# Opening and closing of the convolution backward: a table loaded in two pieces, k^T chunks summed in another order, and a norm correction that lags two tiles

## The chip, the cores and the metric

The kernel runs on one core of a Trainium2 chip. The metric is the device time of one execution in microseconds. All engines of the core are used: TensorE (PE), VectorE (DVE), ScalarE (ACT), GpSimd (POOL) and SyncE (SP). SP only issues transfers here; ACT and POOL issue some beside their own work.

## The reference, cut to what matters

The program is the forward pass and all gradients of four blocks in a row: a long convolution block, an MLP block, and both once more with the same weights. S = 2048 tokens, D = 512 channels, F = 1376 hidden channels, bfloat16.

```python
def _A_ref(q, k, v, shift_k, ssm_k, ssm_D):          # the convolution block
    k_shift = sum over t of 4: k shifted by (3 - t) tokens * shift_k[:, 3 - t]
    kv = k_shift * v
    y = causal convolution of kv with ssm_k along S (by FFT) + kv * ssm_D
    return q * y

def _B_ref(x, w1, b1, w2, b2):                       # the MLP block
    return gelu(x @ w1 + b1) @ w2 + b2

x = x + _A_ref(_layernorm(x), ...)
x = x + _B_ref(_layernorm(x), ...)
x = x + _A_ref(_layernorm(x), ...)
x = x + _B_ref(_layernorm(x), ...)
return x and its gradients for q, k, v, shift_k, ssm_k, ssm_D, w1, b1, w2, b2
```

(The two functions are given in words where the code is long.) What matters below: the gradient of `shift_k` is, for every channel and each of the four shifts, a sum over all tokens of the gradient of `k_shift` times a shifted `k`. The backward of a layernorm subtracts from the gradient of each token two multiples of simple sums over its 512 channels.

## The kernel before, in words

The program has four stages. The forward convolution fills 0 to about 210 us, the forward MLP runs to about 470 us, the backward of the MLP and the norms to about 640 us, and the last 300 us hold the backward of the convolution together with the weight gradients of the MLP.

**The MLP backward** (`phase_mlp`, `b_bwd`, `a_bwd`) works on four slices of 512 tokens, called lanes. Each lane is a Python generator, and `interleave` takes the lane with the least clock next; in this stage a scheduler then orders the instructions of each engine. Lane 3 is the last, and its layer 1 comes last of its layers of that kind. At the end of `b_bwd` four tiles of 128 tokens go through this: eleven matmuls into `gn_ps` (L1133); DVE takes the dot product of `gn_ps` with the normed input `n`, row by row (L1142, output `bb_junk`, sum in `cols`); POOL writes a diagonal matrix `bb_diag` from it (L1145); PE adds that diagonal times `n` to `gn_ps` (L1137), which is the norm correction; DVE then scales and adds (L1138, output `g_sl`). The correction of tile t - 1 is written behind the matmuls of tile t. `a_bwd` then forms `ab_u` and `ab_p` (L1173, L1167, L1171), POOL makes two columns `ab_ab` (L1177 to L1180), ACT applies them to `nb_sl` (L1182), and DVE adds (L1184), and adds into `gy_bf` (L1186, L1188), from which the convolution's backward starts.

**The convolution backward** (`conv_backward`) is written in a fixed order on PE and DVE (`Ordered` keeps the program's order there). It begins with a forward transform of `gy_bf`: DVE folds it (`Fold`; tiles `fold_s`, `fold_t`, `fold_d`), and PE multiplies by a table `tabFb` of 128 partitions x 2 x 2 x 2048, 2 MB in all, which is loaded from `tabF_d` by one transfer on ACT's queue (L729). The columns of the table are cut into five groups (`GROUPS`, of 2, 2, 4, 4, 4 blocks of 128 columns), and `fwd_group` does one group: matmuls into `sp_ps`, evicted by ACT to `GY` (L314). Then come the products with the stored spectra (`Hb`, `KVb`), inverse transforms (`iv_ps`), and for each of four token blocks the gradients of `k_shift` and `v`: `ksb_b`, `Wb`. PE turns them (`gt_ps`, `gr_ps`), and ACT writes `gksT` (L799) and `gr`, a view of `gy_bf` (L796). PE then forms the gradient of k (`gk_ps`), and DVE forms that of `shift_k`: for each of four channel chunks `cc`, and each shift j and half, one `scalar_tensor_tensor` multiplies `gksT` or `gr` by a chunk of k^T and sums along the row. These are 32 instructions, whose product goes to a spare part of `gy_bf` (so the profile calls them `gy_bf<-gksT,kTc` and `gy_bf<-gy_bf,kTc`). The k^T chunks come from `kT_d` on POOL's queue (L810, 544 KB each): chunks 0 and 1 into the buffers that `vb` used (tag `Sg`), chunk 2 into a spare part of `gy_bf`, chunk 3 into a tile of its own. Last comes the gradient of `ssm_k` (`gh_ps`, `Wh`, `ibh`, `gh`).

**The weight gradients** (`weight_grads`) fill the gaps: `conv_backward` yields an amount of room, and the fill generator is stepped until the room is used. A unit of it is sixteen matmuls `dw_ps` on one 128-channel chunk `dw_tm`. In the first half of the units `dw_tm` is loaded through a transposing DMA on SP's queue (L1231 and L55); in the second half PE turns a loaded `dw_fm` (`dw_tp`), ACT evicts it to `dw_tm` (L1246), and DVE sums the rows of `dw_fm` (`b1a`), after which the buffer of `dw_fm` is free. `dw_fm` and `dw_tm` rotate through seven buffers, and up to five units are fetched ahead. Every instruction that goes through `Ordered` has line 55 in the profile; tiles tell them apart.

Of the kernel before, what the change touches and what calls it, by code (L numbers as in the profile page):

```python
# [13 lines left out]
BF16 = mybir.dt.bfloat16  # L14
F32 = mybir.dt.float32
I32 = mybir.dt.int32
P = 128
# [221 lines left out]
def tok_io(nc, sb, ap2d, flipped, i, store=False, eng=None):  # L239
    eng = eng or nc.sync  # L240
    lo = ap2d[i * 512:i * 512 + 256, :].rearrange("(t p) d -> p t d", p=P)
    hi = flipped[i].rearrange("(t p) d -> p t d", p=P)
    for s, d in ((sb[:, 0:2, :], lo), (sb[:, 2:4, :], hi)):
        last = eng.dma_start(out=d, in_=s) if store else eng.dma_start(out=s, in_=d)
    return last
# [43 lines left out]
        return dict(er=T[:, 0], oi=T[:, 1], nei=T[:, 2], orr=T[:, 3])  # L289


def fwd_group(nc, psum, tab, st, g, out, extra=None, m0=0, m1=None):
    k1, base, n = GROUPS[g]
    for mt in range(m0, n if m1 is None else m1):
        cols = slice((base + mt) * P, (base + mt + 1) * P)
        ps = psum.tile([P, 2, 512], F32, name="sp_ps", tag="sp", bufs=2)
        R, Z = [], []
        for qt in range(2):
            C, S = tab[:, 0, qt, cols], tab[:, 1, qt, cols]
            q = slice(qt * 512, (qt + 1) * 512)  # L300
            if k1 in (0, 4):
                R.append((C, st["e"][:, q]))
                Z.append((S, st["o"][:, q]))
            else:
                R += [(C, st["er"][:, q]), (S, st["oi"][:, q])]
                Z += [(C, st["nei"][:, q]), (S, st["orr"][:, q])]
        if extra is not None:
            er, ez = extra(g, mt, st)
            R += er
            Z += ez  # L310
        for b, lst in ((0, R), (1, Z)):
            for i, (a, r) in enumerate(lst):
                nc.tensor.matmul(ps[:, b, :], lhsT=a, rhs=r, start=(i == 0), stop=(i == len(lst) - 1))
        nc.scalar.activation(out=out[:, :, mt - m0, :], in_=ps, func=ACT.Identity)  # L314
# [393 lines left out]
def conv_backward(ctx, nc, tc, dims, consts, dram, res, aps):  # L708
# [16 lines left out]

    H, KV = load_spec("Hb", dram.Hspec, 0), load_spec("KVb", dram.KVspec, 0)
    with tc.tile_pool(name="cb_tabF", bufs=1, side="right", reuse_waits="tile") as tp:
        tabF = tp.tile([P, 2, 2, 2048], BF16, name="tabFb")
        nc.scalar.dma_start(out=tabF, in_=dram.tabF)  # L729
        fg = Fold(nc, tp, None, None, False, res.gy_bf[:, :, :].rearrange("p (i e h) d -> p e i (h d)", i=4, e=2))  # L730
        yield 14.0
        for g, (k1, base, n) in enumerate(GROUPS):
            fwd_group(nc, psum, tabF, fg.streams(k1), g, GY[g])
    tmp = res.gy_bf[:, :, :].rearrange("p (x a b) d -> p x a b d", x=4, a=2)

    with tc.tile_pool(name="cb_w", bufs=1, side="right", reuse_waits="tile") as wp:
# [26 lines left out]
        with tc.tile_pool(name="cb_io", bufs=1, side="right", reuse_waits="tile") as io:  # L763
# [2 lines left out]
            kc3 = io.tile([P, 4 * 544], BF16, name="kTc3")  # L766
            wdiag = io.tile([P, ND, 4, P], BF16, name="wdiag_b")
            dma(out=wdiag, in_=dram.wdiag)
            ksbs = [io.tile([P, 4, D], BF16, name="ksb_b", tag="ksb", bufs=4) for i in range(4)]
            vbs = []  # L770
            for i in range(4):
# [2 lines left out]
                vbs.append(v2[:, i % 2])  # L774
                dma(out=ksbs[i], in_=dram.ks[:, 4 * i:4 * i + 4, :])
                tok_io(nc, vbs[i], v_ap, dram.vB, i, eng=nc.gpsimd)
            tf = res.gy_bf[:, :, :].rearrange("p t d -> p (t d)")
            gr = tf[:, 0:4096].rearrange("p (c i q) -> p c i q", c=ND, i=4)
            nc.vector.memset(gT[:, :, S:S + 16], 0.0)
            for i in range(4):  # L780
                vb, ksb = vbs[i], ksbs[i]
                for h in range(4):
                    gkv = W[h % 2][:, h // 2, 4 + i, :]
                    tt(out=ksb[:, h, :], in0=gkv, in1=ksb[:, h, :], op=ALU.mult)
                    tt(out=gkv, in0=gkv, in1=vb[:, h, :], op=ALU.mult)
                    ps = psum.tile([P, 2, 512], F32, name="gt_ps", tag="sp", bufs=2)
                    for cc in range(ND):
                        cs = slice(cc * P, (cc + 1) * P)
                        nc.tensor.matmul(ps[:, 0, cs], lhsT=gkv[:, cs], rhs=consts.ident if h < 2 else consts.anti,
                                         start=True, stop=True)  # L790
                    if h >= 2:
                        pr = psum.tile([P, 2, 512], F32, name="gr_ps", tag="sp", bufs=2)
                        for cc in range(ND):
                            cs = slice(cc * P, (cc + 1) * P)
                            nc.tensor.matmul(pr[:, 0, cs], lhsT=gkv[:, cs], rhs=consts.ident, start=True, stop=True)
                        nc.scalar.activation(out=gr[:, :, i, P * (h - 2):P * (h - 1)],  # L796
                                             in_=pr[:, 0, :].rearrange("p (c t) -> p c t", c=ND), func=ACT.Identity)
                    t0 = 512 * i + (P * h if h < 2 else 512 - P * (h - 1))
                    nc.scalar.activation(out=gT[:, :, t0:t0 + P],  # L799
                                         in_=ps[:, 0, :].rearrange("p (c t) -> p c t", c=ND), func=ACT.Identity)  # L800
                yield 3.0
                last = tok_io(nc, ksb, out3, dram.o3B, i, store=True, eng=nc.gpsimd)
                if i % 2:
                    with tc.issue_after(last.ins):
                        unflip_rows(nc, aps[f"out_{i // 2}"].flatten_outer_dims(), (dram.o0B, dram.o1B)[i // 2],
                                    eng=nc.gpsimd)
            kcs = [gyp.tile([P, 4096], BF16, name="kTc", tag="Sg", bufs=2)[:, 0:4 * 544] for cc in range(2)]
            kcs += [tf[:, 4096:4096 + 2176], kc3]
            for cc in range(ND):
                dma(out=kcs[cc], in_=dram.kT[:, cc, :, :].rearrange("p i w -> p (i w)"))  # L810
            unflip_rows(nc, out3, dram.o3B, eng=nc.gpsimd)
            for t in range(NT):
                ps = psum.tile([P, 2, 512], F32, name="gk_ps", tag="sp", bufs=2)
# [7 lines left out]
                if t % 4 == 3:  # L821
                    dma(out=out2[(t - 3) * P:(t + 1) * P, :].rearrange("(t p) d -> p t d", p=P), in_=go)
            junk = tf[:, 6272:6272 + 1024].rearrange("p (i q) -> p i q", i=4)
            for cc in range(ND):
                kc = kcs[cc].rearrange("p (i w) -> p i w", i=4)
                for j in range(4):
                    for half in range(2):
                        if half == 0:
                            g_, k_ = gT[:, cc, 0:S].rearrange("p (i q) -> p i q", i=4)[:, :, 0:256], 16 - j
                        else:  # L830
                            g_ = gr[:, cc]
                            k_ = 272 + j
                        nc.vector.scalar_tensor_tensor(out=junk, in0=g_, scalar=1.0, in1=kc[:, :, k_:k_ + 256],
                                                       op0=ALU.mult, op1=ALU.mult, accum_out=gwo[:, half, cc, j:j + 1])
                    yield 2.2
# [61 lines left out]
TS = 4  # L897
# [206 lines left out]
def b_bwd(nc, m, g, l, s, ret, rows, load=None):  # L1104
# [20 lines left out]
        yield 1.0 * k  # L1125
    go = m.gxpool.tile([P, TS, D], BF16, name="g_sl", tag=f"x{s}", bufs=1)
    cols = m.small.tile([P, 2, TS], F32, name="bb_cols", tag="bb_cols", bufs=4)
    pss = {}
    for t in range(TS + 1):
        if t < TS:  # L1130
            ps = pss[t] = m.psum.tile([P, D], F32, name="gn_ps", tag="oo", bufs=4)
            for c in range(NFC):
                nc.tensor.matmul(ps, lhsT=gz[:, c, t * P:(t + 1) * P], rhs=w.w1T[:, c, :], start=(c == 0),  # L1133
                                 stop=(c == NFC - 1))
        if t > 0:
            u, ps = t - 1, pss.pop(t - 1)
            nc.tensor.matmul(ps, lhsT=dg, rhs=n[:, u, :], start=False, stop=True, skip_group_check=True)  # L1137
            nc.vector.scalar_tensor_tensor(out=go[:, u, :], in0=ps, scalar=m.rstd[l][:, s * TS + u:s * TS + u + 1],  # L1138
                                           in1=g[:, u, :], op0=ALU.mult, op1=ALU.add, accum_out=cols[:, 1, u:u + 1])
        if t < TS:  # L1140
            junk = m.small.tile([P, D], BF16, name="bb_junk", tag="bb_junk", bufs=2)
            nc.vector.scalar_tensor_tensor(out=junk, in0=pss[t], scalar=1.0, in1=n[:, t, :], op0=ALU.mult,  # L1142
                                           op1=ALU.mult, accum_out=cols[:, 0, t:t + 1])
            dg = m.small.tile([P, P], BF16, name="bb_diag", tag="bb_diag", bufs=4)
            nc.gpsimd.tensor_scalar(out=dg, in0=m.ident, scalar1=cols[:, 0, t:t + 1], scalar2=-1.0 / D,  # L1145
                                    op0=ALU.mult, op1=ALU.mult)
        if t == 1:
            n2 = m.spool.tile([P, TS, D], BF16, name="nb_sl", tag="n", bufs=m.n_bufs)
            nc.sync.dma_start(out=n2, in_=tok(m.n_d[l - 1], s))
        yield 2.5 if t < TS else 0.2  # L1150
# [304 lines left out]
```

## Time and profile before

| what | value |
|---|---|
| median of 5 runs | 943.59 us (941.13 to 946.16) |
| the profiled execution | 943.52 us, with a span of 941.7 us |
| instructions | 12144 |
| PE, DVE, ACT, POOL busy | 780.1, 733.7, 568.0, 153.8 us |
| mean granted clock of PE | 0.937 |
| 2 MB table, from issue to landing | 11.05 us |

The profile is of one execution. The span runs from the first to the last instruction, and the rest of the execution's time lies around it. In the rows quoted below the first two numbers are the start and the duration in microseconds; in brackets stands how long the engine had been idle before, and what ended that. Matmuls overlap, so the row of a group of them ends a little after the start of the next.

### The profile page before, as it was taken

What the parts mean: (1) busy time and instruction counts of PE and PEld (TensorE: products, weight loads), DVE (VectorE), ACT (ScalarE), POOL (GpSimd) and SP (SyncE); (2) the same over time, 40 slices, a digit from 0 to 9 for tenths busy, and PEclk for the clock granted to TensorE, in tenths of its full rate; (3) what the DMA queues carried; (4) which work ended last, traced back from release to release, by engine and by line L of the source; (5) the groups of instructions that cost most, each with busy time, mean ns of one, the idle gap of its engine ahead of it and who ended that gap; (6) DMA issues with size and microseconds to landing.
All of it is one profiled execution on the core that took longest, in us unless ns stands there. A gap on an engine that the chain in (4) does not pass through costs nothing.

```text
span 941.7 us, 12144 instructions
## 1 busy us (share of the span) xinstructions
PE 780.1 (83%) x4402; PEld 386.0 (41%) x4402; DVE 733.7 (78%) x1203; ACT 568.0 (60%) x742; POOL 153.8 (16%) x274
## 2 busy tenths in 40 slices
PE   3698878964787759639999999977999998987997
PEld 2463323421333324214444444422444445844664
DVE  7748488896898989766647778896389998499974
ACT  5867644637998879579954545622623238634664
POOL 6632210022002010200001122221011304300000
PEclk9999989977989879879999999977999999999999
DMA  6568786213435453575797986688799897862221
GB/s 218 178 251 319 278 281 233 90 46 89 145 121 160 133 159 125 173 195 158 227 303 230 232 233 188 196 189 191 178 262 243 245 383 256 282 202 79 86 83 39
DMA packets 199668, 180.82 MB, mean 192 GB/s; under 512 B 95733, under 2 KB 182456, under 8 KB 199096
## 3 DMA queue, kind: packets, MB, share of 16 engines
q1 hardware_dynamic: 185320, 133.60, 49.6%
q0 software_dynamic: 11968, 40.15, 12.1%
q10 hardware_dynamic: 2320, 6.29, 1.7%
q8 instruction: 34, 0.56, 0.3%
q14 instruction: 26, 0.21, 0.1%
HBM read 84.22 MB, written 82.13 MB: 177 GB/s over the span
## 4 chain that ended last, share of the span: by engine, by line
PE 44%; DVE 24%; ACT 17%; DMA 6%; issue 5%; POOL 3%; SPq 1%; ACTq 0%; DVEq 0%; POOLq 0%
PE dw_ps L55 10%; PE sp_ps L55 7%; PE gn_ps L1133 7%; PE gh_ps L1115 7%; PE iv_ps L55 4%; DVE gy_bf L55 4%; ACT g_z L1089 3%; DVE b1a L55 3%; ACT g_q L1062 2%; ACT g_s L1065 2%; PE gh_ps L55 2%; ACT g_o L1066 2%; DMA kTc<-kT_d 2%; PE z_ps L1087 2%; ACT n_sl L1009 2%
## 5 line engine op out<-in xcount | busy, mean ns | idle before, releaser
L55 PE MATMUL dw_ps<-G,dw_tm 128*128 128x512 bf16 x704 | 168.1, 387 | 8.9 <-ACT dw_tm L1246 8.9
L1087 PE MATMUL z_ps<-nT_sl,w_sb 128*128 128x512 bf16 x352 | 94.4, 428 | 45.3 <-DMA nT_sl<-n_sl 32.3
L1098 PE MATMUL o_ps<-w_sb,h_sl 128*128 128x512 bf16 x352 | 90.4, 397 | 30.0 <-DVE h_sl L1069 27.4
L55 PEld LDWEIGHTS <-dw_tm 128*128 128x128 bf16 x704 | 67.2, 99 | 82.6 <-ACT dw_tm L1246 11.9
L1117 ACT ACTIVATE gz_sl<-gh_ps 128x512 bf16<-128x512 f32 x88 | 50.3, 594 | 57.3 <-PE gh_ps L1115 54.2
L1133 PE MATMUL gn_ps<-w1T_sb,gz_sl 128*128 128x512 bf16 x352 | 81.2, 379 | 1.2 <-DVE gz_sl L1118 1.2
L1115 PE MATMUL gh_ps<-gT_sl,w2T_sb 128*128 128x512 bf16 x352 | 79.1, 379 | 0.0
L1087 PEld LDWEIGHTS <-w_sb 128*128 128x128 bf16 x352 | 37.4, 108 | 100.1 <-issue 53.9
L1089 ACT ACTIVATE g_z<-z_ps,b1col 128x512 bf16<-128x512 f32 x88 | 55.2, 710 | 27.4 <-PE z_ps L1087 27.4
L1098 PEld LDWEIGHTS <-h_sl 128*128 128x128 bf16 x352 | 34.7, 101 | 78.5 <-DVE h_sl L1069 35.5
L1246 ACT ACTIVATE dw_tm<-dw_tp 128x1024 bf16<-128x1024 bf16 x44 | 44.3, 1023 | 36.0 <-PE dw_tp L55 17.9
L1133 PEld LDWEIGHTS <-gz_sl 128*128 128x128 bf16 x352 | 34.4, 98 | 42.8 <-DVE gz_sl L1118 1.7
L1115 PEld LDWEIGHTS <-w2T_sb 128*128 128x128 bf16 x352 | 34.4, 98 | 41.1
L55 DVE TENSOR_REDUCE b1a<-dw_fm 128x1 f32<-128x2048 bf16 x22 | 49.6, 2278 | 0.0
L989 POOL TENSOR_SCALAR rstd<-ln_mv 128x4 f32<-128x4 f32 x16 | 7.6, 474 | 250.2 <-DVE ln_mv L987 161.7
L1145 POOL TENSOR_SCALAR bb_diag<-ident,bb_cols 128x128 bf16<-128x128 bf16 x32 | 22.0, 686 | 158.6 <-DVE bb_junk L1142 149.4
L1118 DVE TENSOR_TENSOR gz_sl<-gz_sl,gpb 128x2048 bf16<-128x2048 bf16 (+1 forms) x24 | 27.3, 1139 | 23.8 <-DMA gpb<-gp_d 12.3
L1065 ACT ACTIVATE g_s<-g_t 128x2048 bf16<-128x2048 bf16 (+1 forms) x24 | 42.8, 1784 | 2.5 <-DVE g_t L1064 2.4
L1062 ACT ACTIVATE g_q<-g_z 128x2048 bf16<-128x2048 bf16 (+1 forms) x24 | 43.2, 1799 | 0.1
L1069 DVE TENSOR_TENSOR h_sl<-g_s,g_z 128x2048 bf16<-128x2048 bf16 (+1 forms) x24 | 27.2, 1132 | 20.1 <-ACT g_s L1065 20.1
L1066 ACT ACTIVATE g_o<-g_t 128x2048 bf16<-128x2048 bf16 (+1 forms) x24 | 42.7, 1779 | 0.0
L1305 ACT ACTIVATE dw_o<-dw_ps 128x512 bf16<-128x512 f32 x22 | 13.1, 596 | 48.3 <-PE dw_ps L55 28.4
(297 smaller groups left out, 1639.5 us busy)
## 6 DMA issues: line engine op xcount, KB each, us to landing
dw_fm<-gz_d SPq DMA_DIRECT2D x22, 512.0 KB, 7.8
h_d<-h_sl SPq DMA_DIRECT2D x16, 512.0 KB, 2.9
gp_d<-g_p SPq DMA_DIRECT2D x16, 512.0 KB, 3.2
nb_sl<-n_d SPq DMA_DIRECT2D x16, 512.0 KB, 4.6
gpb<-gp_d SPq DMA_DIRECT2D x16, 512.0 KB, 4.3
gz_d<-gz_sl SPq DMA_DIRECT2D x16, 512.0 KB, 5.1
n_d<-n_sl SPq DMA_DIRECT2D x12, 512.0 KB, 3.3
Hspec_d<-Hg ACTq DMA_DIRECT2D x8, 512.0 KB, 5.3
```

The lines of the kernel that those rows point to most:

```text
L55: return self.tc.keep_in_program_order(f(*args, **kwargs))
L1062: nc.scalar.activation(out=q, in_=zb, func=ACT.Square)
L1065: nc.scalar.activation(out=sg, in_=t, func=ACT.Sigmoid)
L1066: nc.scalar.activation(out=o, in_=t, func=ACT.Sigmoid, scale=-1.0)
L1087: nc.tensor.matmul(ps, lhsT=w.w1[:, dc, c * P:(c + 1) * P], rhs=nT[:, dc, :], start=(dc == 0), stop=(dc == ND - 1))
L1089: nc.scalar.activation(out=zb[:, c - c0, :], in_=ps, func=ACT.Identity, bias=w.b1col[:, c:c + 1])
L1098: nc.tensor.matmul(ps, lhsT=h[:, c, t * P:(t + 1) * P], rhs=w.w2[:, c, :], start=(c == 0), stop=False)
L1115: nc.tensor.matmul(ps, lhsT=w.w2T[:, dc, c * P:(c + 1) * P], rhs=gT[:, dc, :], start=(dc == 0), stop=(dc == ND - 1))
L1117: nc.scalar.activation(out=gz[:, c, :], in_=ps, func=ACT.Identity)
L1118: nc.vector.tensor_tensor(out=gz[:, c0:c0 + k, :], in0=gz[:, c0:c0 + k, :], in1=gp[:, 0:k, :], op=ALU.mult)
L1133: nc.tensor.matmul(ps, lhsT=gz[:, c, t * P:(t + 1) * P], rhs=w.w1T[:, c, :], start=(c == 0), stop=(c == NFC - 1))
L1246: nc.scalar.activation(out=dst, in_=ps, func=ACT.Identity)
```

## The change

The change has three parts.

1. The table `tabFb` becomes two tiles: its first 512 columns, which are groups 0 and 1, and the other 1536. Each is loaded by a transfer of its own on ACT's queue. `fwd_group` gets an offset for the columns.
2. The loads of k^T chunks 3 and 2 are written earlier in the program (chunk 3 behind the loads of `vb`, chunk 2 behind the first token block), and the sums run over the chunks in the order 3, 2, 0, 1 in place of 0, 1, 2, 3.
3. In layer 1 of lane 3 the norm correction is written two tiles behind the matmuls in place of one. All other lanes keep one.

```diff
-def fwd_group(nc, psum, tab, st, g, out, extra=None, m0=0, m1=None):
+def fwd_group(nc, psum, tab, st, g, out, extra=None, m0=0, m1=None, c0=0):
...
-        cols = slice((base + mt) * P, (base + mt + 1) * P)
+        cols = slice((base + mt) * P - c0, (base + mt + 1) * P - c0)
...
-        tabF = tp.tile([P, 2, 2, 2048], BF16, name="tabFb")
-        nc.scalar.dma_start(out=tabF, in_=dram.tabF)
+        tabF = []
+        for x, w in ((0, 512), (512, 1536)):
+            tabF.append(tp.tile([P, 2, 2, w], BF16, name=f"tabFb{x}"))
+            nc.scalar.dma_start(out=tabF[-1], in_=dram.tabF[:, :, :, x:x + w])
...
-            fwd_group(nc, psum, tabF, fg.streams(k1), g, GY[g])
+            fwd_group(nc, psum, tabF[g > 1], fg.streams(k1), g, GY[g], c0=0 if g < 2 else 512)
...
+            tf = res.gy_bf[:, :, :].rearrange("p t d -> p (t d)")
+            kcs = [None, None, tf[:, 4096:4096 + 2176], kc3]
+
+            def load_kc(cc):
+                dma(out=kcs[cc], in_=dram.kT[:, cc, :, :].rearrange("p i w -> p (i w)"))
...
-            tf = res.gy_bf[:, :, :].rearrange("p t d -> p (t d)")
+            load_kc(3)
...
                 last = tok_io(nc, ksb, out3, dram.o3B, i, store=True, eng=nc.gpsimd)
+                if i == 0:
+                    load_kc(2)
...
-            kcs = [gyp.tile([P, 4096], BF16, name="kTc", tag="Sg", bufs=2)[:, 0:4 * 544] for cc in range(2)]
-            kcs += [tf[:, 4096:4096 + 2176], kc3]
-            for cc in range(ND):
-                dma(out=kcs[cc], in_=dram.kT[:, cc, :, :].rearrange("p i w -> p (i w)"))
+            for cc in range(2):
+                kcs[cc] = gyp.tile([P, 4096], BF16, name="kTc", tag="Sg", bufs=2)[:, 0:4 * 544]
+                load_kc(cc)
...
-            for cc in range(ND):
+            for cc in (3, 2, 0, 1):
...
-    pss = {}
-    for t in range(TS + 1):
+    pss, dgs = {}, {}
+    lag = 2 if l == 1 and s == 3 else 1
+    for t in range(TS + lag):
...
-        if t > 0:
-            u, ps = t - 1, pss.pop(t - 1)
-            nc.tensor.matmul(ps, lhsT=dg, rhs=n[:, u, :], start=False, stop=True, skip_group_check=True)
+        if t >= lag:
+            u, ps = t - lag, pss.pop(t - lag)
+            nc.tensor.matmul(ps, lhsT=dgs[u], rhs=n[:, u, :], start=False, stop=True, skip_group_check=True)
...
-            dg = m.small.tile([P, P], BF16, name="bb_diag", tag="bb_diag", bufs=4)
+            dg = dgs[t] = m.small.tile([P, P], BF16, name="bb_diag", tag="bb_diag", bufs=4)
```

In the built program POOL issues its transfers in the same order as before, PE changes only in the place of one correction, and on SP's queue the two stores of lane 2's gradient move ahead of one transposing load of `dw_tm`. On DVE the order changes in lane 3's tiles and in the 32 sums.

## The prediction

> **What bounds the kernel now.** The profiled execution took 943.5 us: a span of 941.7 us and 1.8 us around it. It stands at the median of the runs shown (943.59), so the sum is made against it directly. First the page: its busy times and its forty slices of 23.5 us.
>
> ```profile
> span 941.7 us, 12144 instructions
> PE 780.1 (83%) x4402; PEld 386.0 (41%) x4402; DVE 733.7 (78%) x1203; ACT 568.0 (60%) x742; POOL 153.8 (16%) x274
> PE   3698878964787759639999999977999998987997
> PEclk9999989977989879879999999977999999999999
> ```
>
> TensorE and VectorE are close, so neither total decides. The three edits lie in slices 26 to 36 (612 to 870 us). There the busy times by stretch, in the order span, PE, PEld, DVE, ACT, POOL, clock, DMA share, GB/s:
>
> ```profile
> 654.00:690.00 36.00, 35.91 (x153) 15.65 (x154) 16.13 (x33) 17.45 (x18) 2.01 (x3) 0.92 0.83 185
> 690.00:770.00 80.00, 80.00 (x390) 37.04 (x389) 75.29 (x100) 23.44 (x33) 13.77 (x21) 1.00 0.98 282
> 800.00:815.00 15.00, 14.70 (x230) 13.18 (x228) 0.79 (x1) 10.02 (x18) 3.22 (x3) 1.00 0.89 283
> 815.00:840.00 25.00, 22.74 (x206) 14.05 (x204) 24.52 (x34) 12.68 (x17) 4.14 (x5) 1.00 0.86 277
> 840.00:870.00 30.00, 21.86 (x143) 12.39 (x141) 29.55 (x40) 10.83 (x15) 0.18 (x1) 0.89 0.25 72
> ```
>
> From 654 to 770 PE is never idle: what PE starts earlier there ends earlier. At 800 to 815 DVE does nothing; at 815 to 870 DVE is full, and PE is idle for 10.4 us with its clock down. The chain of waits names a transfer at both places:
>
> ```profile
> 642.94 11.05 DMA tabFb<-tabF_d
> 654.04 5.31 PE sp_ps L55 x12
> 660.45 20.88 PE sp_ps L55 x96
> 797.78 16.34 DMA kTc<-kT_d
> ```
>
> Last the timeline (start, us, engine, what, and in brackets the idle time before it and who ended it):
>
> ```profile
> 631.39 0.61 PE L1137 MATMUL gn_ps<-nb_sl,bb_diag 128*128 128x512 bf16 x1 [4.02 <-POOL bb_diag L1145]
> 649.04 2.36 DVE L55 TENSOR_TENSOR fold_t<-fold_s 128x2048 bf16<-128x2048 bf16 x2
> 654.04 6.36 PE L55 MATMUL sp_ps<-fold_t,tabFb 128*128 128x512 bf16 x16 [6.89 <-DMA tabFb<-tabF_d]
> 801.21 0.59 ACT L796 ACTIVATE gy_bf<-gr_ps 128x512 bf16<-128x512 f32 x1
> 814.21 1.23 DVE L55 SCALAR_TENSOR_TENSOR gy_bf<-gksT,kTc 128x1024 bf16<-128x1024 bf16 x1 [17.38 <-DMA kTc<-kT_d]
> 838.37 1.94 ACT L1246 ACTIVATE dw_tm<-dw_tp 128x1024 bf16<-128x1024 bf16 x2 [3.32 <-DVE b1a L55]
> 839.45 0.60 PE L55 MATMUL dw_ps<-G,dw_tm 128*128 128x512 bf16 x2 [2.23 <-ACT dw_tm L1246]
> 868.51 5.50 PE L55 MATMUL gh_ps<-tabG,GY 128*128 128x257 bf16 x48 [2.19 <-ACT Wh L871]
> ```
>
> PE waits for the table although its other operand (the first of the two fold_t) is there at about 650.2. DVE waits for a k^T chunk although gksT and gr are there at 801.8; its row sums (b1a) then come late, these free the buffers for ACT's dw_tm, and PE waits for those.
>
> **The change, part by part.**
>
> *K^T order.* Nothing is added; 32 products with 1.22 us each and the row sums between them keep their count, and the order of issues on POOL's queue comes out the same: chunk 3 was already issued at 749.15 (landing 15.5 us later) and chunk 2 at 767.63 (7.0 us later), both in hand by 775. So the "moved" loads are free, and the whole effect is DVE's order 3, 2, 0, 1. The first product now needs gksT, last written by ACT at 800.71 + 0.60 = 801.3. DVE starts at 801.4 in place of 814.2: 12.8 us. Chunks 0 and 1, landing at 814.1, are needed after sixteen products (16 x 1.26 us) and three row sums (3 x 2.2 us), at 828: hidden, with 14 us to spare. What can PE take of it? It is in the gk_ps block until 818.3 in any case. From there to 868.5 it waited 2.23, 1.66, 1.65 and 2.63 us for dw_tm and 2.19 us for Wh, 10.4 in all, and it lost about 4.5 us to half rate after these waits (seven dw_ps at 840.34 took until 843.15 in place of 841.85, and the like up to 865). So PE could win up to 14.9. DVE's row sums come 12.8 earlier, each then before PE's unpaced need of it, except the last, due about a microsecond late: Wh stands behind it on ACT. I take 12.0 us. From 870 to 936 PE is busy for 64.5 of 66 us on work in a fixed order, so the gain reaches the end.
>
> *Table in two pieces.* Removed: one transfer of 2 MB, 11.05 us. Added: 0.5 MB in runs of 1 KB, and 1.5 MB in runs of 3 KB, each with its issue on ACT's queue (0.35 us; ACT's next work waits 9.94 us for sp_ps anyway, so 0.35 costs nothing; uncovered it would cost just that). New waits: piece one waits, as the whole did, for the sixth dw_tm transpose; piece two also for the DMA of the fourth unit's dw_tm, which PE took at 644.16. Behind this wait on ACT stand only the GY evictions, which wait for PE. The size of the pieces is not in the trace. By the table's own rate piece one is 2.8 us; the nearest rows of 512 KB took 4.6 (nb_sl), 7.0 (wdiag_b) and 13.2 (Hb, the same moment but a queue on POOL). I take 5 us, and keep 2.8 to 13. Issued at 642.9, it lands by 648, ahead of fold_t at 650.2. Piece two at 0.75 x 11.05 = 8.3 us, issued some 0.4 us after its dw_tm has landed, is there at about 653; PE needs it after 6.41 us of the first two groups (654.04 to 660.45), at 656.6. So PE starts at 650.2: 3.8 us.
>
> A rule speaks against this part. The Trainium skill (DMA: Bandwidth & Descriptors, Queues, rings and completion order) says that each DMA engine alternates between queues packet by packet. From 615 to 660 us the trace has 144 packets for 2.10 MB on ACT's queue, about 15 KB a turn, against some 320 B on SP's with the transposes (17808 packets, 5.73 MB); with 1 and 3 KB a turn the table loses share. By the trace's busy shares a transpose packet takes 28 ns (68.4% of 45 us x 16 engines / 17808) and one of the table 0.57 us (11.4% likewise), so 1 KB against one such packet is about 36 + 28 ns: 32 turns an engine make 2 us, and piece two, 32 x (107 + 28), 4.3 us. So the rule costs each piece 32 x 28 ns = 0.9 us; piece two is then there at 654, and the sum stays. Its price would show only if a turn were longer than the bytes say, and that goes into the range.
>
> *Lag of two tiles.* The same four corrections; PE's first moves one tile later, and DVE does its row-dot (L1142) for tile 1 ahead of the first L1138. DVE before: waits of 0.61 (626.9) and 0.86 (632.0) for PE. After: the dots come at 624.3, 625.5 and 626.8, so the diagonals are ready in time, but L1184 then stands at 627.4 and its input, ACT's four L1182 from 625.21, ends at 628.14: a new wait of 0.75. Then 0.67 us (L1138) and 0.61 (L1173) in the new order: the last L1173 ends 1.0 us earlier, and with it POOL's ab_ab, ACT's L1182, DVE's fold and the table's issue. On SP the two stores of lane 2 (wait: L1184) move ahead of the fourth transpose: that one goes from about 625 to 630.3, the next from 631.0 to 632.9. The first serves the fifth unit, which PE takes after 681, the second piece one (above): issued at 631.02 it had landed by 637.5, where the DMA rate falls to 0; with these 6.5 us it is there at 639.4, before 641.7. PE's weight-gradient work starts 3 us earlier, but the fold follows in its order, so that is only idle time moved. Bounds: -1 to +1.5 us; I take 1.0.
>
> *Clock.* After 6.89 us of idle PE ran at 427 ns a step until 659.5. The skill (TensorE: Matmul & The Clock Gate, What's actually happening) gives about 3.4 us idle for half rate and as long to recover. PE's gap before sp_ps stays near 3 us or is split by the fourth unit's dw_tm; if full rate held, the first sixteen matmuls would take about 4.3 us with their evictions and not 6.4: 2.1 us more. I leave the slow start in, by the row, and keep the 2.1 for the range.
>
> Sum: 12.0 + 3.8 + 1.0 = 16.8 us; 943.5 - 16.8 = 926.7.
>
> **The rivals.**
> *Opening lost:* small packets or the lane's order make piece two land near 660, or PE meets a late dw_tm in the stage where DMA is 98% busy. For it: 18.8 us for a transpose that ran beside the table. Against: dw_tm come several units ahead. Only the sums: 943.5 - 12.0 = 931.5.
> *The sums' lead turns into a new wait:* dw_fm. SP issued one at 819.4 only after a PE release, and in this busy stretch loads took 9 us; if units of 4.5 us outrun fetches, PE waits at half of its old stalls: 943.5 - 6 - 4.8 = 932.7. Against: fetches run four units (18 us) ahead, and DMA is at 25% after 840.
> *Slower:* piece two alone. At Hb's rate (512 KB in 13.2 us) its 1.5 MB takes 39.6 us; issued at 643.1 it lands at 682.7, PE is held 22.3 us past 660.45, against 12.0 + 0 gained: 953.8. It decides from a landing at 672.5 on, three and a half times the estimate. Against it: the whole 2 MB took 11.05 us at the same moment.
> *The change doesn't do what it says:* true for the loads, which don't move; DVE's order and the table's two transfers do. Both gains failing together leaves 943.5.
>
> **How the numbers follow.** Forecast 0.73 (its own range 922 to 931: sums 10 to 13, opening 2.5 to 7); opening lost 0.12; dw_fm 0.08; no change 0.03; slower 0.04. A difference under 0.3% (2.8 us) cannot be told from none. Range 920 to 935: up to 23.5 us if all bounds fall well, and both middle rivals. Faster 0.93, same 0.03, slower 0.04.
>
> **What would show it.** DVE's 17.38 us wait before the first k^T product shrinks to about 5, none of it for kTc; ACT's waits for b1a between 820 and 860 go from 12.4 us to 2 or less, PE's for dw_tm likewise; sp_ps starts some 5 us earlier with no wait for the first piece. Wrong if sp_ps<-fold_d waits for the second piece, if PE waits for DMA dw_fm or dw_tm, or if the gain at sp_ps is gone by 770.

## The result and the profile after

The changed kernel took 936.43 us (median of 43 runs, 926.52 to 945.58). The kernel before, run beside it, took 941.86 us (78 runs, 936.99 to 952.98). The ratio is 0.9915, with a 95% interval from 0.9901 to 0.9929: 8.0 us of 943.5 are gained, where 16.8 were forecast. Ratios leave out runs over 1.5% above the fastest of the same kernel; because this change also widens the spread of its runs, their range is given beside every ratio.

The profiled execution took 941.21 us, so it is one of the slower runs of the changed kernel; a second profile, of a run at 937.2 us, follows among the experiments. From its page: the busy times have hardly changed. In the slices of 23.5 us, the 29th (658 to 681 us) has gone from 9 to 5 tenths of PE, and the 36th and 37th (822 to 869 us) from 8 and 7 to 9 and 8. The low clock, 7 in slices 27 and 28 before, is now 8 in slice 27 and 7 in slice 29.

```profile
span 939.4 us, 12147 instructions
PE 779.9 (83%) x4402; PEld 386.5 (41%) x4402; DVE 733.4 (78%) x1203; ACT 568.1 (60%) x742; POOL 152.6 (16%) x274
PE   3698878964778749639999999986599998898998
PEclk9798989977999779878999999989799999999999
```

The same five stretches as before, again in the order span, PE, PEld, DVE, ACT, POOL, clock, DMA share, GB/s:

```profile
654.00:690.00 36.00, 22.54 (x97) 9.95 (x98) 6.66 (x15) 12.18 (x13) 0.57 (x1) 0.81 0.76 167
690.00:770.00 80.00, 80.00 (x373) 36.23 (x371) 75.05 (x105) 22.22 (x31) 14.68 (x22) 1.00 0.95 263
800.00:815.00 15.00, 12.57 (x138) 8.88 (x137) 10.99 (x19) 11.81 (x21) 4.81 (x6) 1.00 0.85 270
815.00:840.00 25.00, 25.00 (x320) 19.63 (x318) 24.65 (x32) 15.25 (x23) 6.76 (x8) 1.00 0.88 282
840.00:870.00 30.00, 26.38 (x202) 15.90 (x201) 29.53 (x38) 15.47 (x22) 0.78 (x1) 1.00 0.56 145
```

PE loses 13.4 us of work between 654 and 690 (35.91 to 22.54 busy), and gains 2.3 and 4.5 us between 815 and 870. DVE now works from 800 on (10.99 us in place of 0.79), and the clock in the last row is back at 1.00. The timeline shows both halves (start, duration, engine, what, and in brackets the idle time and who ended it):

```profile
642.28 0.58 ACTq L731 DMA_DIRECT2D tabFb<-tabF_d  x1
643.60 0.57 ACTq L731 DMA_DIRECT2D tabFb<-tabF_d  x1
649.80 1.89 PE L55 MATMUL sp_ps<-fold_t,tabFb 128*128 128x512 bf16 x8 [1.53 <-DVE fold_t L55]
651.93 1.94 PE L55 MATMUL sp_ps<-fold_t,tabFb 128*128 128x512 bf16 x8 [0.25 <-ACT GY L314]
667.46 0.61 PE L55 MATMUL sp_ps<-fold_d,tabFb 128*128 128x512 bf16 x1 [13.59 <-DMA tabFb<-tabF_d]
808.58 1.23 DVE L55 SCALAR_TENSOR_TENSOR gy_bf<-gksT,kTc 128x1024 bf16<-128x1024 bf16 x1 [2.86 <-ACT gksT L807]
866.73 5.50 PE L55 MATMUL gh_ps<-tabG,GY 128*128 128x257 bf16 x48 [0.29 <-ACT Wh L880]
```

The first piece is never waited for, and `sp_ps` starts 4.2 us earlier than before (649.80, 654.04). But the second piece, issued at 643.60, is there only at 667.46, 23.9 us later. Before, this second part of `sp_ps` began at 660.45. So the opening is behind by 7 us, and with the slow start of PE after the wait (its first steps take some 0.43 us each and not 0.21, and the granted clock from 654 to 690 is 0.81 in place of 0.92) by 8.7 us (the first `iv_ps` at 701.32, before at 692.61). The first k^T product then starts 5.6 us earlier than before although everything ahead of it is late, and waits for `gksT`, not for a transfer. The waits of PE from 815 to 870:

```profile
PE dw_ps L55 <- ACT dw_tm L1256: 3.3, 2, 1.7
PE gh_ps L55 <- ACT Wh L880: 0.3, 1, 0.3
```

10.4 us of waiting have become 3.6, and ACT no longer waits for a row sum (`b1a`) in this stretch.

### The profile page after: what moved, and what is told of

The parts are those of the page before. It is cut to its first block, busy times and chain, and to the rows that moved or that the text cites. A ratio compares the mean times of both kernels' runs of the same rounds, so it can differ in the third digit from the quotient of the medians.

```text
span 939.4 us, 12147 instructions
## 1 busy us (share of the span) xinstructions
PE 779.9 (83%) x4402; PEld 386.5 (41%) x4402; DVE 733.4 (78%) x1203; ACT 568.1 (60%) x742; POOL 152.6 (16%) x274
```

## The experiments

One measure serves for all profiles. The stretch *opening* runs from lane 2's four ACT instructions on `nb_sl` (L1182 before) to the first `iv_ps`; the stretch *rest* from there to the end of the span. What lies ahead of the opening moves by up to 5 us from run to run (the opening starts at 621 to 626 us) and says nothing about the change.

| kernel | opening, us | rest, us | table issued after the opening's start | range of runs, us |
|---|---|---|---|---|
| before | 67.4 | 249.1 | 17.7 | 937.0 to 953.0 (78 runs) |
| changed, first profile | 75.8 | 238.1 | 16.8 and 18.1 | 926.5 to 945.6 |
| changed, second profile | 75.5 | 239.0 | 16.8 and 18.3 | 937.2 |
| sums alone | 71.6 | 238.1 | 17.7 | 928.4 to 934.9 |
| table alone | 70.9 | 249.1 | 17.5 and 19.1 | 940.7 to 960.8 |
| sums and lag | 65.4 | 238.1 | 16.8 | 928.7 to 931.3 |
| sums and lag, run again | 65.2 | 238.6 | 16.8 | 925.8 to 932.0 |
| contiguous pieces | 60.7 | 263.2 | 16.8 and 18.3 | 924.5 to 950.6 |
| contiguous pieces, run again | 78.7 | 241.5 | 16.8 and 18.4 | 927.1 to 947.3 |
| one transfer, runs of 4 KB | 68.7 | 249.1 | 17.6 | 941.2 to 957.4 |
| one transfer, runs of 1 KB | 72.3 | 251.5 | 17.6 | 946.6 to 950.5 |
| two pieces, runs of 1 KB | 75.2 | 238.0 | 16.8 and 18.0 | 929.9 to 941.4 |
| changed, plain `dw_tm` loads | 62.0 | 238.5 | 16.8 and 17.4 | 925.4 to 927.5 |
| contiguous pieces, plain loads | 62.0 | 240.9 | 16.8 (both) | 923.8 to 930.7 |

**The parts one by one.** *Sums alone* is the kernel before with only the order of the k^T chunks changed:

```diff
-            for cc in range(ND):
+            for cc in (3, 2, 0, 1):
```

(with the loads written as in the change; POOL issues them in the same order.)

> The kernel before with the k^T order alone (sums 3, 2, 0, 1; table in one transfer, lag of one tile). Theory A (what the change lost, it lost at the table; the sums give their 12.0 us in full): 943.5 - 12.0 = about 931, ratio 0.987, the first k^T product at about 801 in place of 814, sp_ps where it was (654). Rival B (part of the sums' gain turns into another wait before the end, and the table's share is smaller than it looks): 936 to 938, ratio 0.993, with new waits of PE or ACT after 840.

Measured: 930.16 us, ratio 0.9873 (0.9852 to 0.9894), which is 12.0 us of 943.5. Its profile, the first k^T product in the timeline and the table's wait:

```profile
656.79 5.92 PE L55 MATMUL sp_ps<-fold_t,tabFb 128*128 128x512 bf16 x16 [10.76 <-DMA tabFb<-tabF_d]
802.13 1.23 DVE L55 SCALAR_TENSOR_TENSOR gy_bf<-gksT,kTc 128x1024 bf16<-128x1024 bf16 x1 [2.87 <-ACT gksT L805]
```

The product comes at 802.13 although the table happened to land late in this run (15.5 us after its issue, and 11.05 in the profile of before). Theory A holds for the sums; no new wait takes back any of it.

*Table alone* is the kernel before with `tabFb` as two tiles and two transfers, and nothing else of the change:

```diff
-        tabF = tp.tile([P, 2, 2, 2048], BF16, name="tabFb")
-        nc.scalar.dma_start(out=tabF, in_=dram.tabF)
+        tabF = []
+        for x, w in ((0, 512), (512, 1536)):
+            tabF.append(tp.tile([P, 2, 2, w], BF16, name=f"tabFb{x}"))
+            nc.scalar.dma_start(out=tabF[-1], in_=dram.tabF[:, :, :, x:x + w])
...
```

> The kernel before with the table in two pieces alone. In the profile of the changed kernel the first piece is there by 649.8 and the second only at 667.5, about 24 us after its issue. Theory A (short runs of 1 and 3 KB lose the DMA engines to the transposes, whatever else is changed): piece two lands 660 to 668 here too, the products with the second piece wait for it by 5 to 14 us, and the kernel is slower than before by 2 to 8 us: 946 to 951, ratio 1.002 to 1.009. Rival C (the lag moves the transposes on SP's queue onto the table's time, and only so the second piece is late): without the lag it lands by 655, and the time is 3 to 4 us below before: 940, ratio 0.996.

Measured: 946.57 us, ratio 1.0052 (1.0017 to 1.0087), so slower by half a per cent. In the timeline of its profile the second piece is issued at 642.00 and waited for:

```profile
642.00 0.57 ACTq L731 DMA_DIRECT2D tabFb<-tabF_d  x1
659.63 0.61 PE L55 MATMUL sp_ps<-fold_d,tabFb 128*128 128x512 bf16 x1 [7.66 <-DMA tabFb<-tabF_d]
```

It was there 17.6 us after its issue, in a kernel without the lag. Rival C, that only the lag's reordering of SP's queue makes the piece late, is out. Whether the lag adds to it is open: with it piece two takes 22.7 us and more in four of five profiles (below).

*Sums and lag*: the changed kernel with one table transfer.

```diff
-        for x, w in ((0, 512), (512, 1536)):
-            tabF.append(tp.tile([P, 2, 2, w], BF16, name=f"tabFb{x}"))
-            nc.scalar.dma_start(out=tabF[-1], in_=dram.tabF[:, :, :, x:x + w])
+        tabF = tp.tile([P, 2, 2, 2048], BF16, name="tabFb")
+        nc.scalar.dma_start(out=tabF, in_=dram.tabF)
```

> The changed kernel with the table in one transfer again (sums and lag stay). Theory A (the table in two pieces costs time): faster than the changed kernel's 0.9915: 943.5 - 12.0 - 1.0 = 930.5, ratio 0.986. Rival B (the sums give less): ratio 0.990 to 0.993. Rival C (the lag makes any table late): sp_ps starts 3 us or more behind 654 here too, and the ratio is 0.990.

Measured: 930.43 us, ratio 0.988 (0.9862 to 0.9898). The same kernel once more:

> The kernel with the new order of the sums and the lag and with the table in one transfer once more, on the same chip as the contiguous pieces: 930.4 us, ratio 0.988, runs within 4 us of each other; sp_ps starts when the table lands, 10 to 15 us after its issue. Rival: a spread as with the contiguous pieces (15 us), if stalls strike every version with a k^T order that leaves the last 70 us free.

Measured: 929.82 us, ratio 0.9868 (0.9834 to 0.9902), runs from 925.8 to 932.0, so a little wider than the 4 us that were expected and far from 15. The timeline of the first of these profiles:

```profile
641.75 0.35 ACTq L729 DMA_DIRECT2D tabFb<-tabF_d  x1
651.77 6.27 PE L55 MATMUL sp_ps<-fold_t,tabFb 128*128 128x512 bf16 x16 [3.64 <-DMA tabFb<-tabF_d]
```

This is the version to keep: it beats the kernel before, and with a ratio of 0.987 to 0.988 also the changed kernel at 0.9915. Against the sums alone (0.9873) the lag cannot be told in the time; in the trace it is there, as the table is issued 16.8 us after the opening's start in place of 17.7.

**Why the second piece is late.** First the changed kernel again, for a second profile.

> The changed kernel once more, unaltered, for a second profile: its runs lie between 926.5 and 945.6, the profiled one at 941.2 with 13.6 us of waiting for piece two. Theory E (what differs from run to run is how long the table's second piece and the loads behind it take to land, since the DMA engines stall for some microseconds in some runs): if this run takes 926 to 930, the wait for piece two is under 3 us; if 935, about 8; everything up to the first piece and from the k^T sums on stays as it was. Rival F (the spread comes from elsewhere, for instance the forward stage): the wait is again 12 us or more whatever the time.

```profile
639.28 0.56 ACTq L731 DMA_DIRECT2D tabFb<-tabF_d  x1
661.97 0.61 PE L55 MATMUL sp_ps<-fold_d,tabFb 128*128 128x512 bf16 x1 [12.67 <-DMA tabFb<-tabF_d]
```

The run took 937.18 us, 4.0 less than the first profile, and its wait is nearly the same (12.67 against 13.59 us). The 4 us lie ahead of the opening, which starts at 620.95 in place of 625.53. So between these two runs rival F is right, and theory E explains none of their difference; what they agree on is a piece two that needs 23 to 24 us.

The first theory was the length of the runs, that is of the stretches of bytes that lie together in a partition: 1 and 3 KB in the pieces, against one of 16 KB. If so, pieces that are each one run per partition (4 and 12 KB) should land in time:

```diff
-    dram.tabF = drampool.tile([P, 2, 2, 2048], BF16, name="tabF_d")
+    dram.tabF = [drampool.tile([P, 2, 2, w], BF16, name=f"tabF_d{w}") for w in (512, 1536)]
...
-    nc.gpsimd.dma_start(out=dram.tabF, in_=tabF)
+    for d, x, w in zip(dram.tabF, (0, 512), (512, 1536)):
+        nc.gpsimd.dma_start(out=d, in_=tabF[:, :, :, x:x + w])
...
-            nc.scalar.dma_start(out=tabF[-1], in_=dram.tabF[:, :, :, x:x + w])
+            nc.scalar.dma_start(out=tabF[-1], in_=dram.tabF[len(tabF) - 1])
```

> The changed kernel with one thing more: the table is stored in memory as two tensors, so that each piece is one run per partition (4 KB and 12 KB in place of four runs of 1 KB and four of 3 KB); one more store on POOL's queue in the forward stage. Theory A (the length of the runs decides): piece one lands by 648, piece two by 655, group 2 follows group 1 without a wait, sp_ps starts at about 650: 943.5 - 16.8 = 926.7, ratio 0.982. Rival D (two transfers side by side, or the moment of their issue, make the second late, whatever its runs): piece two lands at 660 or later, ratio 0.990 as for the changed kernel.

In the timeline the opening is the one that I had forecast, with no wait for either piece:

```profile
649.13 1.89 PE L55 MATMUL sp_ps<-fold_t,tabFb 128*128 128x512 bf16 x8 [1.38 <-DVE fold_t L55]
653.40 0.38 PE L55 MATMUL sp_ps<-fold_d,tabFb 128*128 128x512 bf16 x1 [0.20 <-ACT GY L314]
685.55 1.89 PE L55 MATMUL iv_ps<-Yb,tabIb 128*128 128x512 bf16 x8
```

The opening takes 60.7 us, 6.7 less than before. Yet this run took 950.55 us: 14.1 us more than before are spent in the rest (25 us more than in the other kernels with the new order of the sums), on loads that came late. From the waits between 655 and 800 (total, times, longest):

```profile
PE iv_ps L55 <- DVE Yb L55: 16.9, 5, 8.9
DVE pr_t L55 <- DMA Hb<-Hspec_d: 15.0, 3, 9.4
DVE pr_t L55 <- DMA KVb<-KVspec_d: 11.6, 1, 11.6
```

Six runs lay at 924.5, 927.2, 938.9, 941.0, 942.2 and 950.6. It was run again:

> The kernel with contiguous pieces once more, for its spread (924.5 to 950.6) and a second profile. Theory E (its opening is as forecast, and what it loses it loses to stalled loads behind it): group 2 follows group 1 without a wait of 2 us in this profile too; if the profiled run takes under 930 there is no wait of DVE for Hb or KVb over 2 us, if it takes 937 or more these waits and PE's for Yb make up the difference. Rival I (the late loads were an accident of one run): all runs at 924 to 928.

```profile
643.68 0.33 ACTq L732 DMA_DIRECT2D tabFb<-tabF_d  x1
669.25 0.61 PE L55 MATMUL sp_ps<-fold_d,tabFb 128*128 128x512 bf16 x1 [15.59 <-DMA tabFb<-tabF_d]
```

Now piece two, in runs of 12 KB, took 25.6 us, longer than in the changed kernel. Theory E's opening is refuted as well as rival I: the same kernel can have the best and the worst opening of all. Over its ten runs the median is 940 us. Both profiles are of its slowest runs, and none shows what a run at 924 to 933 us does differently. But long runs do not save the second piece for certain.

The reverse test keeps one transfer and shortens its runs. In one kernel a gap behind every 512 columns of the tile makes it sixteen runs of 1 KB, in the other a gap in the stored table makes it four of 4 KB.

```diff
-        tabF = tp.tile([P, 2, 2, 2048], BF16, name="tabFb")
-        nc.scalar.dma_start(out=tabF, in_=dram.tabF)
+        tabF = tp.tile([P, 2, 2, 4, 528], BF16, name="tabFb")
+        nc.scalar.dma_start(out=tabF.rearrange("p f q x w -> p (f q x) w")[:, :, 0:512],
+                            in_=dram.tabF.rearrange("p f q (x w) -> p (f q x) w", x=4))
```

> The kernel before with the table still in one transfer, but into a tile with a gap behind every 512 columns, so that it moves in 16 runs of 1 KB per partition in place of one of 16 KB. Theory A (short runs lose the DMA engines to the transposes): the table lands at 662 or later, sp_ps starts 8 us or more behind 654, 951 us or more, ratio 1.008 or more. Rival D (two transfers, not short runs, were late): lands at about 654, ratio 1.000.

```diff
-    dram.tabF = drampool.tile([P, 2, 2, 2048], BF16, name="tabF_d")
+    dram.tabF = drampool.tile([P, 4, 1, 2064], BF16, name="tabF_d")
...
-        nc.scalar.dma_start(out=tabF, in_=dram.tabF)
+        nc.scalar.dma_start(out=tabF[:, :, :, :].rearrange("p f q (x w) -> p (f q) x w", x=1),
+                            in_=dram.tabF[:, :, :, 0:2048])
```

> The kernel before with its one table transfer in four runs of 4 KB per partition (a gap behind each row of the stored table). One run of 16 KB took 11.05 us in the first profile (15.5 us where only the sums were changed), 16 runs of 1 KB took 16.3 us. Theory A (the shorter the runs, the later): between these, sp_ps starts 12 to 15 us after the issue, 943 to 947, ratio 1.002. Theory H (runs of 3 to 4 KB fare worst): the table lands 20 us or more after its issue, sp_ps starts 8 us late or more, ratio 1.009 or more.

The timelines, 1 KB first:

```profile
639.03 0.59 ACTq L730 DMA_DIRECT2D tabFb<-tabF_d  x1
655.30 6.04 PE L55 MATMUL sp_ps<-fold_t,tabFb 128*128 128x512 bf16 x16 [11.54 <-DMA tabFb<-tabF_d]
```

```profile
640.77 0.59 ACTq L730 DMA_DIRECT2D tabFb<-tabF_d  x1
653.29 6.20 PE L55 MATMUL sp_ps<-fold_t,tabFb 128*128 128x512 bf16 x16 [7.86 <-DMA tabFb<-tabF_d]
```

16.3 us from issue to use with runs of 1 KB, 12.5 with 4 KB, and 10.0 to 15.5 with 16 KB (11.05 in the profile of before). In the time: 948.43 us and 1.007 (1.0044 to 1.0096) for 1 KB, 943.33 us and 1.0014 (0.9995 to 1.0032) for 4 KB. So runs of 1 KB do cost, 4 to 9 us by the interval (in the profile 4.9 us in the opening and 2.4 in the rest); at 4 KB no cost is clear of the noise. Theory A has the sign, but not the size that it needs. One transfer of 2 MB in the shortest runs is done 7 us sooner than piece two alone with its 1.5 MB.

That left the count of transfers. In the next kernel both pieces move in runs of 1 KB (a gap behind every 512 columns of the stored table):

```diff
-    dram.tabF = drampool.tile([P, 2, 2, 2048], BF16, name="tabF_d")
+    dram.tabF = drampool.tile([P, 4, 4, 528], BF16, name="tabF_d")
...
-            nc.scalar.dma_start(out=tabF[-1], in_=dram.tabF[:, :, :, x:x + w])
+            nc.scalar.dma_start(out=tabF[-1].rearrange("p f q (x w) -> p (f q) x w", w=512),
+                                in_=dram.tabF[:, :, x // 512:(x + w) // 512, 0:512])
```

> The changed kernel with its second piece also in runs of 1 KB (12 per partition in place of four of 3 KB; the stored table has a gap behind every 512 columns). The changed kernel's piece two took 23 to 24 us for 1.5 MB in both profiles, though the whole 2 MB in runs of 1 KB took 16.3 us. Theory A (the shorter the runs, the later): piece two lands even later than in the changed kernel, group 2 waits 14 us or more, ratio 0.992 or more. Theory H (runs of 1 KB keep the rate of 16.3 us for 2 MB, it is the runs of 3 KB that fare badly here): piece two lands some 14 us after its issue, near 657, group 2 waits 4 us or less, about 930, ratio 0.987. Rival D (two transfers beside each other are slow, whatever their runs): group 2 waits 10 us or more, ratio 0.991.

```profile
644.41 0.62 ACTq L732 DMA_DIRECT2D tabFb<-tabF_d  x1
667.62 0.61 PE L55 MATMUL sp_ps<-fold_d,tabFb 128*128 128x512 bf16 x1 [11.40 <-DMA tabFb<-tabF_d]
```

23.2 us again, at 936.4 us and 0.9937 (0.9905 to 0.9968). Theory H is wrong, and rival D right in its numbers: as the second of two transfers, the 1.5 MB took 23.2 us in runs of 1 KB, 17.6 to 23.9 in runs of 3 KB, and 25.6 or at most 10.2 in runs of 12 KB.

**What holds it up.** Last, the transposing loads of `dw_tm` on SP's queue are replaced by plain loads of the same bytes. Half of the weight gradients is then left unturned, so these two kernels serve only to find the cause.

```diff
-            sync.dma_start_transpose(out=tms[k], in_=m.h_d[layers[i]][:, c, :])
+            sync.dma_start(out=tms[k].rearrange("p t f -> p (t f)"), in_=m.h_d[layers[i]][:, c, :])
```

> The changed kernel with the 22 transposing loads of dw_tm made plain loads of the same bytes (so half of the weight gradients is left unturned; the instructions of all engines stay). Theory A (it is the transposes beside them that hold up the short runs): piece two lands by 653, group 2 follows group 1 without a wait, and the runs lie within 4 us of each other near 926, ratio 0.982. Rival G (the table's short runs are slow by themselves, or the spectra's loads hold them up): group 2 still waits 5 us or more, ratio 0.990.

```profile
649.51 5.30 PE L55 MATMUL sp_ps<-fold_t,tabFb 128*128 128x512 bf16 x16 [4.26 <-DVE fold_t L55]
655.06 0.38 PE L55 MATMUL sp_ps<-fold_d,tabFb 128*128 128x512 bf16 x1 [0.25 <-ACT GY L314]
```

No piece is waited for, with the runs of 1 and 3 KB as they were. 925.63 us, four runs between 925.4 and 927.5, ratio 0.9837 (0.9804 to 0.987). The same with contiguous pieces:

> The changed kernel with contiguous pieces and with plain loads of dw_tm (half of the weight gradients left unturned). With transposes the contiguous pieces took 924.5 to 950.6, in the slowest run because Hb, KVb and tabIb were up to 23 to 28 us under way. Theory E1 (these stalls come with the transposes): every run within 4 us of 925, no DVE wait for Hb or KVb over 2 us. Rival E2 (the stage from 655 to 740 asks for more than the DMA engines give once the opening is earlier): the spread of 15 us or more stays.

925.55 us, 923.8 to 930.7, ratio 0.984 (0.9797 to 0.9883); DVE waits 3.5 us in all for Hb and none for KVb. The range is 7 us and not 4, but the stalls of 10 us and more are gone. So the transposing loads are a necessary part of the late piece and of the stalled spectra, and by these few runs of most of the spread. They do not make the spread alone: with one transfer beside them, the kernels with four to ten runs spread by 3 to 7 us (one run at 957.4 aside). Nor is it shown that the transposing itself does it. The transposes also move in far smaller packets (in the rows below, 1045 packets under 512 B against 128), and no run takes the two apart.

What they do to the others can be read in the DMA view. For 648 to 660 us, each row is a queue (q1: SP, q10: ACT, thus the table, q0: POOL) with packets, MB, and the time of its packets as a share of 16 engines x 12 us. The changed kernel, then the same with plain loads:

```profile
DMA packets 1496, 1.57 MB, mean 131 GB/s; under 512 B 1045, under 2 KB 1131, under 8 KB 1496
q10 hardware_dynamic: 273, 0.82, 56.7%
```

```profile
DMA packets 1664, 4.40 MB, mean 367 GB/s; under 512 B 128, under 2 KB 768, under 8 KB 1629
q10 hardware_dynamic: 365, 1.07, 24.2%
```

A packet of the table was under way for 0.567 x 192 us / 273 = 399 ns on average in the first and 127 ns in the second (packets of different queues overlap: with 52.4% for q1 and 8.6% for q0 the first adds up to 118%). And the contiguous kernel in its two profiles, the good opening first:

```profile
DMA packets 6381, 3.85 MB, mean 321 GB/s; under 512 B 5420, under 2 KB 6060, under 8 KB 6316
q10 hardware_dynamic: 80, 0.79, 15.5%
```

```profile
DMA packets 795, 2.03 MB, mean 170 GB/s; under 512 B 558, under 2 KB 558, under 8 KB 682
q10 hardware_dynamic: 125, 1.39, 79.3%
```

Same program, same moment: 372 ns a packet against 1218 ns, and 321 GB/s against 170. There is not more to carry in the second. Nor is every packet slow: in the trace's list of packets the median one of 12 KB took 464 ns in the good stretch and 467 in the bad one, but 15 of the 113 in the bad one took more than 1 us, up to 10.7, and these hold 69% of the time. In the changed kernel 25 of 267 took more than 1 us, up to 3.2, and hold 54%; with plain loads none of 349 did. (With runs of 1 KB it was many packets: 432 of 2048 took over three times the median of 46 ns.)

The second transfer does not make this stretch. The kernel before has it too, from 652 to 656 us, just behind the last packet of its table, which started at 650.96:

```profile
DMA packets 429, 0.35 MB, mean 89 GB/s; under 512 B 365, under 2 KB 365, under 8 KB 429
```

With the sums alone it came earlier (139 GB/s from 644 to 648), and there the one transfer met it and took 15.5 us. What sets it off is open; no run isolates it. That the second of two transfers mostly meets it (five of six profiles), and one transfer mostly not (one of six), is shown by the landings. Why is argued from the packets: piece two's first starts only behind the last of piece one, in the changed kernel at 648.06 us, 4.5 us after its issue, so that 0.52 MB of the table had moved by 648 us, where one transfer had moved 1.03. In the good contiguous profile piece two's packets started between 646.12 and 649.63, ahead of the stretch.

## Why the prediction was right and wrong

The direction and one of the three terms were right, and the time was half missed: 926.7 us was forecast, with 922 to 931 as the forecast's own range; the measurement (936.4, or 943.5 x 0.9915 = 935.5) lies just beyond the upper end of the full range (the better end of the interval, 934.2, is inside). The kernel reaches the forecast only in its best runs, of which no profile was kept. The terms as measured one by one fit the whole: 12.0 + 1.0 (the lag, from the trace) - 4.9 (the table alone) = 8.1 us, against 8.0.

**K^T order, 12.0 us: right.** Alone it measures 12.0 us (10.0 to 14.0), and in the traces the rest of the kernel is 11.0 us shorter (249.1 to 238.1), also in the changed kernel. Each step shows: DVE's first product waits 2.9 us for `gksT` in place of 17.4 for a transfer, chunks 0 and 1 are hidden, PE's waits fall from 10.4 to 3.6 us, and the clock holds 1.00 from 840 to 870. PE waits for no `dw_fm`, so this rival did not come.

**Lag, 1.0 us: right in size, not provable in the time.** The table is issued 0.98 us earlier relative to lane 2.

**Slow start, 2.1 us kept out of the sum:** it was there to be had. The first sixteen matmuls took from 649.80 to 653.87, 4.1 us and not 6.4, after a gap of 1.5 us in place of 6.9. In the other profiles gaps up to 2.9 us left it at 4.1 us, and gaps of 3.2 us and more made it 5.3 to 6.4, so the limit lies near the idle time for half rate that the prediction weighed. The good contiguous opening gained 6.7 us, close to 3.8 + 1.0 + 2.1.

**Table in two pieces, 3.8 us gained: this step failed.** The half on piece one held (in hand by 649.80). The step that was wrong reads "Piece two at 0.75 x 11.05 = 8.3 us", with the 0.9 us that the packet rule added. It took 23.9 us in the first profile, and 17.6 to 25.6 in four of the five others with two pieces beside transposes; once, with contiguous pieces, it was at hand within 10.2. Against a need at 653.9 this is a wait of 13.6 us. Alone the edit costs 4.9 us (0.52%); the changed kernel is 3 to 4 us slower than the same without it. The prediction had a hint of it: the 18.8 us of a transpose beside the table stood in it, as a point for the rival. It took one transfer's 11.05 us and scaled them by bytes, as if the DMA engines gave the later piece what they had given the whole. But the second transfer did most of its work from 648 us on, and there they gave less: in the profile of before they fell to 89 GB/s from 652 to 656 us, when the table's packets were through, and it was transposes and spectra (Hb with 13.2 us) that lost time. The prediction used Hb's row as the upper bound of piece one and for the slower rival, and not for piece two.

The rule weighed there (the Trainium skill, DMA: Bandwidth & Descriptors, Queues, rings and completion order: queues take turns packet by packet) agrees in sign. With one transfer, shortening the runs from 16 to 1 KB cost 0.7% in the time. But the run does not single out the turns, since short packets also took longer by themselves (16 median packets of 1 KB 16 x 46 = 736 ns, one of 16 KB 614), and the page's packet can hold several descriptors, so no run shows how many of the trace's packets make a turn. By the rule, runs of 12 KB should hardly have suffered, and in one profile of two they took 25.6 us. The error was the price of a turn, an average (28 ns for a transpose's packet, 107 ns for 3 KB) over 45 us: in the bad stretch the 3 KB took 399 ns on average, through a few packets that took microseconds.

**The rivals.** "Opening lost" came, and worse than priced: not 3.8 and 1.0 us forgone, but a loss of 8.7 us in the profile and some 4 in the mean. It named the cause by half ("small packets"). The slower case did not come: piece two stayed short of 672.5, the latest in any profile being 669.25. Without the sums' 12 us it would have been slower, as the table alone shows. All three signs given for a wrong forecast appeared: the wait of `sp_ps<-fold_d`, the loss at `sp_ps` by 770, and a wait of PE for the DMA of `dw_tm` (2.0 us at 643.63, which cost nothing here, since PE then still waited 1.5 us for `fold_t`).

## What to carry to other kernels

When a transfer is cut so that its first part comes early, price the last part by the stretch of time in which it will run, and not by the bytes of the whole: look at what the DMA engines deliver in the ten microseconds behind the old landing. Where transposing loads run there, one landing in one profile is a sample of something that varies by 15 us, so ask several profiles before building on it. Reordering consumers so that the operands already in hand come first, on the other hand, cost nothing here and gave just what the waits had promised.

## What the runs showed of the hardware that was not expected

Beside transposing loads the DMA engines fell for some 4 to 12 us to a fraction of their rate, with packets of several queues under way: to 131 GB/s (changed kernel) and 170 (contiguous pieces, second profile) from 648 to 660 us, where the same contiguous kernel in its other profile moved 321 and the changed kernel with plain loads 367. The kernel before has such a stretch as well (89 GB/s from 652 to 656 us). The mean packet of the table then took three times as long (1218 against 372 ns in the contiguous kernel, 399 against 127 in the changed one), while the median of 12 KB hardly moved (467 against 464): a few packets took up to 10.7 us. The stretch met piece two in five of the six profiles with two pieces, and came behind it in the sixth. The runs of these kernels spread by 11 to 26 us; without the transposes they spread by 2 and 7, in four runs each. What starts the stretch, and whether the transposing or its small packets do it, stays open.
